# One pool pair for attention and experts, and a fill between indirect transfers in a row

## The chip, the cores and the metric

The kernel runs on one core of one Trainium2 chip. The metric is the device time of one execution in microseconds, the median of three runs. The engines are named as the profile names them: PE is TensorE's matrix multiply and PEld its weight load, DVE is VectorE, ACT is ScalarE, POOL is GpSimd, SP is the engine whose queue issues most plain DMA transfers. SBUF is the on-chip memory of 128 partitions; PSUM is the accumulator memory that TensorE writes, in banks of 512 f32 columns, eight of them.

## The reference

Two stages: a linear attention with a norm, and a mixture of eight experts in which each token goes to one expert.

```python
def _attn_ref(q, k, v, g_norm):            # q, k, v: 8 batches x 8 heads x 576 x 64
    kv = np.einsum('bhsd,bhse->bhde', k, v)
    out = np.einsum('bhsd,bhde->bhse', q, kv)
    rms = np.sqrt(np.mean(out * out, axis=-1, keepdims=True) + 1e-06)
    return (out / rms * g_norm).astype(np.float32)

def _moe_ref(x, w_gate, w1, w2):           # x: 4608 tokens x 512; 8 experts, 512 -> 1024 -> 512
    logits = x @ w_gate
    expert_idx = np.argmax(logits, axis=1)
    # gate_w: the softmax probability of the chosen expert
    for e in range(E):
        mask = expert_idx == e
        xe = x[mask]
        h = np.maximum(xe @ w1[e], 0.0)
        out[mask] = gate_w[mask, None] * (h @ w2[e])
```

## The kernel before

The kernel walks over 36 tiles of 128 tokens (`for s in range(36)`): products with q, norm, gate logits. Each finished row (512 f16 values, its token number and its gate weight) is sent to a scratch table in DRAM, sorted by expert, with an indirect DMA from GpSimd (`scatter`). Then each expert's rows come back with indirect DMAs, 128 rows at a time (`gather`), are transposed, go through both layers, and are sent to their places in the output with a third kind of indirect DMA (`put`). Each expert has up to five such tiles (`CT = 5`); rows beyond that form a "left" job at the end. For experts 0 and 1 the first three tiles (`AT = 3`) are done early, while the last scatters still run: these are `j0` and `j1`, and jobs 0 and 1 of the main loop are their remaining two tiles.

```python
def gather(xe, rows, src=None):
    return nc.gpsimd.indirect_dma_start(out=xe.bitcast(I32), in_=xs.ap() ..., in_offset=IndirectOffsetOnAxis(ap=rows, axis=0), ...)

def put(view, idx, ys):
    nc.gpsimd.indirect_dma_start(out=view, out_offset=IndirectOffsetOnAxis(ap=idx, axis=0), in_=ys, ...)
```

Attention and the early batches take their tiles from one SBUF pool and one PSUM pool:

```python
with (
    tc.manual_schedule(engines=by_hand),
    tc.tile_pool(name="pattn", bufs=1) as PA,
    tc.tile_pool(name="psattn", bufs=1, space=bass.MemoryType.PSUM) as PSA,
):
    ...                                     # attention, routing, j0, most of j1   (cut)
    W[2].stage1(hold=True)                  # loads of expert 2's weights, 2 MB each
    W[2].stage2(hold=True)
    for m in range(4):
        j1.one(m, ("op", "kvp")[m % 2])
        ...
    yp0 = PSA.tile([128, D], F32, tag="qtp", bufs=1, name="yp")
    j1.two(0, yp0)
    j1.done(0, yp0)                         # ys = yp * gate weight, then put(...)
    yp = PSA.tile([128, 2, D], F32, tag="kvp", bufs=1, name="yp")
    for t in (1, 2):
        j1.two(t, yp[:, t - 1, :])
        j1.done(t, yp[:, t - 1, :])
```

The experts use a second pair of pools, which takes over the memory of the first:

```python
with (
    tc.tile_pool(name="pffn", bufs=1) as PF,
    tc.tile_pool(name="psffn", bufs=1, space=bass.MemoryType.PSUM) as PSF,
):
    class Job:
        def flip(self, t):                  # transpose a gathered tile
            if t == 0:
                self.xt = PF.tile([128, 4, nt * 128], F16, tag=f"xt{nt}", bufs=2, name="xt")
                ...
            xp = PSF.tile([128, 4, 128], F16, tag="xp", bufs=2, name="xp")
            ...                             # 4 transposes on PE, a DVE copy xt <- xp, the row numbers
        def one(self, ws, f):               # first layer: 4 matmuls, then relu on ACT into ht
            hp = PSF.tile([128, wd], F32, tag="hp", bufs=3, name="hp")
            ...
        def two(self, t):                   # second layer: 8 matmuls, scaling on DVE, put on POOL
            yp = PSF.tile([128, D], F32, tag="yp", bufs=3, name="yp")
            ...
            ys = PF.tile([128, D], F32, tag="ys", bufs=8, name="ys")
            nc.vector.tensor_scalar(ys, yp, self.xe[t][:, 514:516].bitcast(F32), None, op0=ALU.mult)
            put(self.views[t], self.idx[:, t:t + 1], ys)

    with tc.manual_schedule(engines=by_hand):
        def next_row(n, t, job, ws, f):     # wait for a relu of this job, then gather for job n
            nc.gpsimd.tensor_copy(tick2, job.ht[:, f, c:c + 1])
            gather(jobs[n].xe[t], rowi[:, order[n], t:t + 1])

        for t in range(CT):
            gather(jobs[2].xe[t], rowi[:, 2, t:t + 1])
        for t in range(2):
            jobs[0].flip(t)
        for n in range(len(order)):
            for ws in range(job.halves):
                for f in range(8):
                    job.one(ws, f)
                    if coming and ...:      next_row(n + 2, coming.pop(0), job, ws, f)
                    if ws == job.halves - 1 and f >= 2 and flips:
                        nxt.flip(flips.pop(0))
                    ...                     # DVE: W[n + 1].half1, conversion of the next w1; SP: load of W[n + 2]
            for kk in range(max(job.nt, 4)):
                if kk < job.nt:
                    job.two(kk)
                ...                         # ACT: W[n + 1].half2, conversion of the next w2
                if n == 2 and kk == 1:
                    left_over_table()       # some 25 small DVE operations
```

Within one `manual_schedule` block each engine's order is that of the program. The two blocks are separate, and their orders are merged: the gathers of job 2, written after the puts of `j1`, stand before some of them in the GpSimd queue.

Of the kernel before, what the change touches and what calls it, by code (L numbers as in the profile page):

```python
# [28 lines left out]
def kernel(  # L29
# [165 lines left out]

    def gather(xe, rows, src=None):
        return nc.gpsimd.indirect_dma_start(  # L197
            out=xe.bitcast(I32),
            out_offset=None,
            in_=xs.ap() if src is None else src,  # L200
            in_offset=IndirectOffsetOnAxis(ap=rows, axis=0),
            bounds_check=E * N - 1,
            oob_is_err=False,
        )
# [8 lines left out]
    def put(view, idx, ys):  # L213
        nc.gpsimd.indirect_dma_start(  # L214
            out=view,
            out_offset=IndirectOffsetOnAxis(ap=idx, axis=0),
            in_=ys,
            in_offset=None,
            bounds_check=N - 1,
            oob_is_err=False,  # L220
        )
# [6 lines left out]
    with (  # L228
        tc.manual_schedule(engines=by_hand),
        tc.tile_pool(name="pattn", bufs=1) as PA,  # L230
        tc.tile_pool(name="psattn", bufs=1, space=bass.MemoryType.PSUM) as PSA,
    ):
# [43 lines left out]
        def heads(s):  # L276

            qp[s] = PA.tile([128, 2, 4, 64], F32, tag="qp", bufs=5, name="qp")
            (b0, j0), (b1, j1) = tokens(s)
            if b0 == b1:  # L280
                tv = ld["q", b0][:, :, 64 * j0:64 * j0 + 128]
                nc.gpsimd.tensor_copy(qp[s], tv.rearrange("p i (c d) -> p c i d", c=2))  # L282
            else:
                for c, (b, j) in enumerate(tokens(s)):
                    nc.gpsimd.tensor_copy(
                        qp[s][:, c, :, :], ld["q", b][:, :, 64 * j:64 * j + 64]
                    )
# [232 lines left out]
        class Route:  # L520
# [69 lines left out]
            def scatter(self, t):  # L590
                put_xs = nc.gpsimd.indirect_dma_start(  # L591
                    out=xs_views[9 * self.P + self.g0 + t],
                    out_offset=IndirectOffsetOnAxis(ap=self.sli[:, t:t + 1], axis=0),
                    in_=xgs[self.P, self.g0][:, t, :].bitcast(I32),
                    in_offset=None,
                )
                if self.P < 3:
                    known.append(put_xs.ins.name)
# [185 lines left out]
        yp0 = PSA.tile([128, D], F32, tag="qtp", bufs=1, name="yp")  # L784
        j1.two(0, yp0)
        j1.done(0, yp0)
        yp = PSA.tile([128, 2, D], F32, tag="kvp", bufs=1, name="yp")
        for t in (1, 2):
            j1.two(t, yp[:, t - 1, :])
            j1.done(t, yp[:, t - 1, :])  # L790


    with (
        tc.tile_pool(name="pffn", bufs=1) as PF,
        tc.tile_pool(name="psffn", bufs=1, space=bass.MemoryType.PSUM) as PSF,
    ):

        def left_over_table():

            ovr = PF.tile([128, 8], F32, tag="ovr")  # L800
            nc.vector.tensor_sub(ovr, cnt, dlt)
            nc.vector.tensor_scalar(ovr, ovr, float(CAP), 0.0, op0=ALU.subtract, op1=ALU.max)
            thr = PF.tile([128, 8, 32], F32, tag="thr")
# [4 lines left out]
            ov = PF.tile([128, 8], F32, tag="ov")  # L808
            nc.vector.reduce_sum(ov, thr, axis=AXX)
            oi = PF.tile([128, 8], F32, tag="oi")  # L810
            zero8 = PF.tile([128, 8], F32, tag="zero8")
            nc.vector.memset(zero8, 0.0)
            nc.vector.tensor_tensor_scan(oi, ov, zero8, 0.0, op0=ALU.add, op1=ALU.add)
            cm = PF.tile([128, 32, 8], F32, tag="thr")
            nc.vector.tensor_tensor(cm, _bc(oi, 1, 32), _bc(tcol, 2, 8), op=ALU.is_le)
            te = PF.tile([128, 32], F32, tag="te")
            nc.vector.reduce_sum(te, cm, axis=AXX)
            nc.vector.tensor_tensor(cm, cm, _bc(ov, 1, 32), op=ALU.mult)
            tk = PF.tile([128, 32], F32, tag="tk")
# [3 lines left out]
            e8 = PF.tile([128, 8], F32, tag="e8")  # L823
            nc.vector.tensor_scalar(e8, eoff, 1.0 / N, None, op0=ALU.mult)
            nc.vector.tensor_tensor(cm, _bc(te, 2, 8), _bc(e8, 1, 32), op=ALU.is_equal)
            cd = PF.tile([128, 32, 8], F32, tag="cd")
            nc.vector.tensor_tensor(cd, cm, _bc(dlt, 1, 32), op=ALU.mult)
            td = PF.tile([128, 32], F32, tag="td")
# [16 lines left out]

        class Job:


            def __init__(self, xe, w, okm, bgm, views):
# [3 lines left out]
                self.halves = 2 if self.cols > 512 else 1  # L853

            def flip(self, t):

                nt, xe = self.nt, self.xe
                if t == 0:
                    self.xt = PF.tile(
                        [128, 4, nt * 128], F16, tag=f"xt{nt}", bufs=2, name="xt"  # L860
                    )
                    self.idx = PF.tile([128, nt], I32, tag=f"idx{nt}", bufs=3, name="idx")
                xp = PSF.tile([128, 4, 128], F16, tag="xp", bufs=2, name="xp")
# [9 lines left out]
            def one(self, ws, f):  # L873
                if ws == 0 and f == 0:
                    self.ht = PF.tile(
                        [128, 8, self.cols], F16, tag=f"ht{self.nt}", bufs=2, name="ht"
                    )
                wd = self.cols // self.halves
                hp = PSF.tile([128, wd], F32, tag="hp", bufs=3, name="hp")
                for kk in range(4):  # L880
# [8 lines left out]
                    self.ht[:, f, ws * wd:(ws + 1) * wd], hp, ACTF.Relu  # L889
                )  # L890

            def two(self, t):
                yp = PSF.tile([128, D], F32, tag="yp", bufs=3, name="yp")
                for f in range(8):
                    nc.tensor.matmul(  # L895
                        yp, self.ht[:, f, t * 128:(t + 1) * 128], self.w.w2[:, f, :],
                        start=(f == 0), stop=(f == 7),
                    )
                ys = PF.tile([128, D], F32, tag="ys", bufs=8, name="ys")
# [5 lines left out]
        def left_over(t, t0, view):  # L905
# [5 lines left out]
            okm = PF.tile([128, 1], F32, tag="okm", bufs=2, name="okm")  # L911
            nc.vector.tensor_tensor(okm, pcol, nvf[:, bass.ds(t, 1)], op=ALU.is_lt)
            bgm = PF.tile([128, 1], F32, tag="bgm", bufs=2, name="bgm")
            nc.vector.tensor_scalar(bgm, okm, -BIG, BIG, op0=ALU.mult, op1=ALU.add)
            gi = PF.tile([128, 1], I32, tag="gi", bufs=2, name="gi")
# [7 lines left out]
        with tc.manual_schedule(engines=by_hand):  # L923
            jobs = []
            for n, e in enumerate(order):
                if e == "left":
                    jobs.append(None)
                    continue
                t0 = AT if n < 2 else 0
                x0 = 2 * AT + 2 * n if n < 2 else (10, 0, 5)[(n - 2) % 3]  # L930
                jobs.append(Job(
                    xe_bufs[x0:x0 + CT - t0], W[n], valid[:, e, t0:CT], bigm[:, e, t0:CT],
                    out_views[e * CT + t0:(e + 1) * CT],
                ))

            tick2 = PF.tile([128, 1], F16, tag="tick2")

            def next_row(n, t, job, ws, f):

                c = ws * (job.cols // job.halves)  # L940
                nc.gpsimd.tensor_copy(tick2, job.ht[:, f, c:c + 1])  # L941
                gather(jobs[n].xe[t], rowi[:, order[n], t:t + 1])

            for t in range(CT):
                gather(jobs[2].xe[t], rowi[:, 2, t:t + 1])
            for t in range(2):
                jobs[0].flip(t)

            for n in range(len(order)):
                job = jobs[n]  # L950
                if n == 4:
                    jobs[E] = left_over(0, 3 * CT, out_views[E * CT])
                    W[E] = jobs[E].w
                nxt = jobs[n + 1] if n + 1 < len(order) else None
                flips = list(range(nxt.nt)) if nxt is not None else []
                coming = list(range(CT)) if 0 < n < len(order) - 3 else []
                for ws in range(job.halves):
                    for f in range(8):
                        job.one(ws, f)
                        step = 8 * ws + f  # L960
                        if coming and (step % 3 == 0 if n > 1 else f < 5):
                            next_row(n + 2, coming.pop(0), job, ws, f)
                        if ws == job.halves - 1 and f >= 2 and flips:
                            nxt.flip(flips.pop(0))
                        if n > 0 and ws == 0 and f % 2 == 1 and nxt is not None:
                            W[n + 1].half1(nc.vector, f // 2)
                            if f == 7 and n + 2 < len(order):
                                W[n + 2].stage1()
                for kk in range(max(job.nt, 4)):
                    if kk < job.nt:  # L970
                        job.two(kk)
                    if n > 0 and kk < 4 and nxt is not None:
                        W[n + 1].half2(kk)
                        if kk == 3 and n + 2 < len(order):
                            W[n + 2].stage2()
                    if n == 2 and kk == 1:
                        left_over_table()

        nov = nc.values_load(tabi[0:1, 1, 7:8], min_val=0, max_val=NOV)
        with tc.If(nov > 1):  # L980
            with tc.For_i(1, nov) as t:
                job = left_over(t, 3 * CT, out_views[E * CT + 1])
                job.w.stage1()
                job.w.stage2()
                for kk in range(4):
                    job.w.half1(nc.vector, kk)
                    job.w.half2(kk)
                job.flip(0)
                for f in range(8):
                    job.one(0, f)  # L990
                job.two(0)
# [28 lines left out]
```

## Time and profile before

| | |
|---|---|
| time, median of 3 | 305.62 us (304.78 to 306.7) |
| span of the profiled execution | 328.7 us |
| busy: PE, PEld | 276.4 us (84%), 191.5 us (58%) |
| busy: DVE, ACT, POOL | 157.9 us (48%), 165.8 us (50%), 164.3 us (50%) |
| DMA moved | 85.73 MB, mean 261 GB/s |
| indirect transfers on POOL | 36 scatters to the table, 41 gathers (34, 6 and 1), 41 puts |

The profile is of one execution, which was longer than the timed ones. Busy shares are averages over stages with different limits: attention lasts until some 143 us, the early batches until 171, the experts from 180 on. Lines of the timeline have start and duration in us, engine, source line, operation, output and input, and in brackets the idle time of the engine before it with what ended it. "issue" is a wait that the profile shows no cause for; "remote" is a release whose origin the trace doesn't name. For an indirect DMA the line covers the work of GpSimd, not the landing of the data. In the chain of waits each piece is a start, a duration, and the work or transfer that was waited for.

### The profile page before, as it was taken

To read this page: it belongs to the slowest core of one execution; us is meant where nothing else is said; L and a number is where in the kernel's file an instruction comes from. 1 tells how busy PE (TensorE), PEld (TensorE's weight loads), DVE (VectorE), ACT (ScalarE), POOL (GpSimd) and SP (SyncE) were. 2 spreads that over 40 slices of the span, in tenths; PEclk is the share of its full clock that TensorE was granted. 3 is DMA by queue.
4 is the path that set the end of the run, shared out by engine and by line. 5 is a ranking of instruction groups with operands and counts; after the bars stand their busy time and mean duration, and the time that the engine had idled before them with its cause. 6 is when DMAs were issued, how large, how long until landed. Compare 5 with 4: busy or idle time off the path is not lost. (4 is left out here: it accounts for less than half of the span.)

```text
span 328.7 us, 7210 instructions
## 1 busy us (share of the span) xinstructions
PE 276.4 (84%) x2832; PEld 191.5 (58%) x2832; DVE 157.9 (48%) x424; ACT 165.8 (50%) x353; POOL 164.3 (50%) x238
## 2 busy tenths in 40 slices
PE   8897989979996967258952999799979999999992
PEld 3586877868885856224521665456446474665651
DVE  0034856844784747524321280787453354546130
ACT  1245766643764656427800356455434466473831
POOL 9511253764365663742773088327685484305051
PEclk9999999985999898769995899999997999999999
DMA  7999878949599767320695029997779597987330
GB/s 283 373 391 389 323 259 313 397 121 394 169 401 398 299 205 277 99 76 26 223 379 221 2 82 350 390 352 272 302 257 402 154 368 290 312 322 254 150 123 33
DMA packets 34883, 85.73 MB, mean 261 GB/s; under 512 B 3868, under 2 KB 4125, under 8 KB 34848
## 3 DMA queue, kind: packets, MB, share of 16 engines
q1 hardware_dynamic: 26592, 65.10, 54.9%
q0 software_dynamic: 6976, 18.96, 15.8%
q10 hardware_dynamic: 1280, 1.20, 1.1%
q8 instruction: 23, 0.38, 0.5%
q14 instruction: 12, 0.10, 0.1%
HBM read 71.71 MB, written 15.50 MB: 265 GB/s over the span
## 5 line engine op out<-in xcount | busy, mean ns | idle before, releaser
L888 ACT ACTIVATE ht<-hp 128x320 f16<-128x320 f32 (+2 forms) x120 | 49.1, 419 | 81.2 <-PE hp L881 70.4
L881 PE MATMUL hp<-xt,w1e 128*128 128x320 f16 (+2 forms) x480 | 72.2, 299 | 11.8 <-DVE xt L868 5.9
L214 POOL DMA_INDIRECT out_dram<-ys,idx x41 | 42.7, 1042 | 71.3 <-DVE ys L900 61.7
L881 PEld LDWEIGHTS <-w1e 128*128 128x128 f16 x480 | 45.7, 100 | 29.0 <-issue 7.4
L895 PE MATMUL yp<-w2e,ht 128*128 128x512 f16 x280 | 61.9, 379 | 0.0
L368 PE MATMUL op<-kvs,qts 128*128 128x144 f32 (+1 forms) x320 | 50.3, 315 | 3.2 <-DVE xg L408 1.9
L591 POOL DMA_INDIRECT xs_scratch<-xg,sli x36 | 35.4, 983 | 22.8 <-issue 22.2
L895 PEld LDWEIGHTS <-ht 128*128 128x128 f16 x280 | 27.3, 98 | 31.4
L368 PEld LDWEIGHTS op<-kvs,qts 128*128 128x128 f32 (+1 forms) x320 | 41.3, 193 | 6.8 <-DVE xg L408 2.3
L900 DVE TENSOR_SCALAR ys<-yp,xe 128x512 f32<-128x512 f32 x35 | 26.0, 750 | 39.9 <-PE yp L895 38.7
L197 POOL DMA_INDIRECT xe<-xs_scratch,rowi x34 | 35.7, 1049 | 9.4 <-issue 6.0
L394 DVE TENSOR_REDUCE ms<-sq 128x8 f32<-128x512 f32 x36 | 24.6, 684 | 22.0 <-ACT sq L389 18.4
L389 ACT ACTIVATE sq<-op 128x512 f32<-128x512 f32 x36 | 21.5, 596 | 25.6 <-PE op L368 22.6
L192 ACT CAST w2e<-ws 128x1024 f16<-128x1024 f32 x32 | 31.2, 1041 | 1.5 <-DMA ws<-in_moe_w_dram 1.5
L868 DVE COPY xt<-xp 128x512 f16<-128x512 f16 x35 | 14.7, 421 | 34.4 <-PE xp L865 21.1
L346 PE MATMUL qtp<-cf,qp 128*128 128x128 f32 x144 | 24.2, 293 | 1.5 <-POOL qp L282 1.5
L299 PE MATMUL kvp<-v,k 64*64 64x64 f32 x1152 | 24.4, 227 | 1.3 <-DMA v<-in_v_dram 0.7
L180 DVE TENSOR_SCALAR w1e<-ws,g 128x1024 f16<-128x1024 f32 x31 | 21.9, 755 | 6.8 <-DMA ws<-in_moe_w_dram 6.8
L408 DVE TENSOR_TENSOR xg<-op,rinv 128x512 f16<-128x512 f32 x36 | 24.5, 681 | 0.0
L299 PEld LDWEIGHTS kvp<-v,k 64*64 64x64 f32 x1152 | 20.3, 138 | 7.0 <-issue 7.0
L353 ACT COPY qts<-qtp 128x512 f32<-128x512 f32 x36 | 21.1, 585 | 6.4 <-PE qtp L346 6.3
L282 POOL COPY qp<-q 128x512 f32<-128x512 f32 x32 | 19.6, 626 | 9.3 <-DMA q<-in_q_dram 9.2
(115 smaller groups left out, 275.9 us busy)
## 6 DMA issues: line engine op xcount, KB each, us to landing
ws<-in_moe_w_dram SPq DMA_DIRECT2D x16, 2048.0 KB
q<-in_q_dram SPq DMA_DIRECT2D x8, 1152.0 KB
k<-in_k_dram SPq DMA_DIRECT2D x7, 1152.0 KB
v<-in_v_dram SPq DMA_DIRECT2D x7, 1152.0 KB
ws<-in_moe_w_dram SPq DMA_DIRECT2D x4, 1024.0 KB
k<-in_k_dram SPq DMA_DIRECT2D x2, 576.0 KB
v<-in_v_dram ACTq DMA_DIRECT2D x2, 576.0 KB
out_dram<-ys,idx POOLq DMA_INDIRECT x41
```

The lines of the kernel that those rows point to most:

```text
L192: copy(self.w2[:, 2 * kk:2 * kk + 2, :], self.s2[:, 2 * kk:2 * kk + 2, :])
L197: return nc.gpsimd.indirect_dma_start(out=xe.bitcast(I32), out_offset=None, in_=xs.ap() if src is None else src, in_offset=IndirectOffsetO ...
L214: nc.gpsimd.indirect_dma_start(out=view, out_offset=IndirectOffsetOnAxis(ap=idx, axis=0), in_=ys, in_offset=None, bounds_check=N - 1, oob_ ...
L299: nc.tensor.matmul(kvst[b][64 * ip:64 * ip + 64, c, 64 * i2:64 * i2 + 64], ld["k", b][ps, i, cs], ld["v", b][ps, i, cs], start=(j == 0), s ...
L368: nc.tensor.matmul(op[ts, c, 144 * i2:144 * i2 + 144], qts[s][:, 2 * i2 + c, ts], kvs[:, 2 * c + i2, :], start=True, stop=True,)
L394: nc.vector.reduce_sum(ms, sq, axis=AXX)
L408: nc.vector.tensor_tensor(xg[:, r, 0:512].rearrange("p (i h c n) -> p c i h n", c=2, i=2, h=2), ox, _bc(r4, 4, 64), op=ALU.mult,)
L591: put_xs = nc.gpsimd.indirect_dma_start(out=xs_views[9 * self.P + self.g0 + t], out_offset=IndirectOffsetOnAxis(ap=self.sli[:, t:t + 1], a ...
L881: nc.tensor.matmul(hp, self.w.w1[:, kk, f * 128:(f + 1) * 128], self.xt[:, kk, ws * wd:(ws + 1) * wd], start=(kk == 0), stop=(kk == 3),)
L888: nc.scalar.activation(self.ht[:, f, ws * wd:(ws + 1) * wd], hp, ACTF.Relu)
L895: nc.tensor.matmul(yp, self.ht[:, f, t * 128:(t + 1) * 128], self.w.w2[:, f, :], start=(f == 0), stop=(f == 7),)
L900: nc.vector.tensor_scalar(ys, yp, self.xe[t][:, 514:516].bitcast(F32), None, op0=ALU.mult)
```

## The change

It does two things. First, the second pair of pools goes away. The experts' tiles take turns in attention's buffers, under its tags, and all of it stands in one `manual_schedule` block, so the order on each engine is that of the program from start to end. The transposes of job 0 are placed before the last product of `j1`. Nothing has to be handed from pool to pool any more. Second, a function `spaced` puts a fill of 128x576 f16 on GpSimd between indirect transfers that follow one another; a call of `heads` (which itself has GpSimd copy a tile) resets it.

```diff
+    breath = P_const.tile([128, 576], F16, tag="breath")
+    near = []
+    def spaced():
+        if near:
+            nc.gpsimd.memset(breath, 0.0)
+        near[:] = [1]
     def gather(xe, rows, src=None):
+        spaced()
     def put(view, idx, ys):
+        spaced()
             def scatter(self, t):
+                spaced()
         def heads(s):
+            near.clear()
-    with (
-        tc.manual_schedule(engines=by_hand),
-        tc.tile_pool(name="pattn", bufs=1) as PA,
-        tc.tile_pool(name="psattn", bufs=1, space=bass.MemoryType.PSUM) as PSA,
-    ):
+    PA = ctx.enter_context(tc.tile_pool(name="pa", bufs=1))
+    PSA = ctx.enter_context(tc.tile_pool(name="psa", bufs=1, space=bass.MemoryType.PSUM))
+    with tc.manual_schedule(engines=by_hand):
 ...
-                    self.xt = PF.tile([128, 4, nt * 128], F16, tag=f"xt{nt}", bufs=2, name="xt")
-                xp = PSF.tile([128, 4, 128], F16, tag="xp", bufs=2, name="xp")
+                    self.xt = PA.tile([128, 4, nt * 128], F16, tag="k", bufs=2, name="xt")
+                if t % 2 == 0:
+                    self.xp = PSA.tile([128, 2, 8, 128], F16, tag="kvp", bufs=1, name="xp")
+                xp = self.xp[:, t % 2, 0:4, :]
 ...
-                if ws == 0 and f == 0:
-                    self.ht = PF.tile([128, 8, self.cols], F16, tag=f"ht{self.nt}", bufs=2, name="ht")
+                if ws == 0 and f % 4 == 0:
+                    self.ht.append(PA.tile([128, 4, self.cols], F16, tag="vq"[f // 4], bufs=2 + f // 4, name="ht"))
-                hp = PSF.tile([128, wd], F32, tag="hp", bufs=3, name="hp")
+                if f % 2 == 0:
+                    self.hp = PSA.tile([128, 2, 512], F32, tag="op", bufs=2, name="hp")
+                hp = self.hp[:, f % 2, 0:wd]
 ...
+        banks = ["qtp", "misc"]
-                yp = PSF.tile([128, D], F32, tag="yp", bufs=3, name="yp")
+                banks.reverse()
+                yp = PSA.tile([128, D], F32, tag=banks[0], bufs=1, name="yp")
-                ys = PF.tile([128, D], F32, tag="ys", bufs=8, name="ys")
+                ys = PA.tile([128, D], F32, tag="qp", bufs=5, name="ys")
 ...
-            for t in range(CT):
-                gather(jobs[2].xe[t], rowi[:, 2, t:t + 1])
-            for t in range(2):
-                jobs[0].flip(t)
+        for t in range(AT):
+            if t == 2:
+                for u in range(2):
+                    jobs[0].flip(u)
+            banks.reverse()
+            yp = PSA.tile([128, D], F32, tag=banks[0], bufs=1, name="yp")
+            j1.two(t, yp)
+            j1.done(t, yp)
+        for t in range(CT):
+            gather(jobs[2].xe[t], rowi[:, 2, t:t + 1])
```

The rest of the diff renames pools (`PF` to `PA`), moves lines to the outer block, and cuts the lines of `j1.two` that stood in the first block.

## The prediction

> **What bounds the kernel now.** I read the chain of waits first, because it tells which wait ends last. From 220 us to the end its pieces are the matmuls of the experts (`hp`, `yp`), with the GpSimd queue beside them. Its first pieces are something else:
>
> ```profile
> 173.82 1.00 DMA out_dram<-ys,idx
> 174.82 0.30 issue
> 175.12 3.03 DMA out_dram<-ys,idx
> ...
> 178.78 0.42 DVE xt L868
> ```
>
> The first copy into `xt`, a buffer of the second pair of pools, waits for the landing of the last scatter to the output, which reads `ys`, a buffer of the first pair. Neither needs the other's data: this is memory handed from one pool to the next. The timeline of the same stretch shows what it costs and why the scatter is so late:
>
> ```profile
> 157.80 1.05 POOL L197 DMA_INDIRECT xe<-xs_scratch,rowi  x1 [1.08 <-issue]
> ...
> 168.81 1.89 PE L505 MATMUL yp<-w2e,early 128*128 128x512 f16 x8 [1.88 <-issue]
> ...
> 172.34 0.75 DVE L512 TENSOR_SCALAR ys<-yp,xe 128x512 f32<-128x512 f32 x1 [3.59 <-remote]
> ...
> 175.12 0.98 POOL L214 DMA_INDIRECT out_dram<-ys,idx  x1 [0.30 <-issue]
> 178.78 0.42 DVE L868 COPY xt<-xp 128x512 f16<-128x512 f16 x1 [5.68 <-DMA out_dram<-ys,idx]
> ...
> 179.72 2.53 PE L881 MATMUL hp<-xt,w1e 128*128 128x256 f16 x11 [5.91 <-DVE xt L868]
> ```
>
> TensorE ends the early batches at 170.70 (168.81 + 1.89) and starts the next expert at 179.72, with eight transposes between: a hole of 9.0 us. Meanwhile GpSimd works through indirect transfers in a row, one each 1.31 us, five of them gathers that are not urgent (those of expert 2, first used at 190). Next the table of windows, for the clock (columns: busy time of PE, PEld, DVE, ACT, POOL, then the granted clock, DMA share, GB/s):
>
> ```profile
> 171.00:180.00 9.00, 0.94 (x10) 0.65 (x10) 1.76 (x5) 0.00 (x0) 4.01 (x4) 0.64 0.72 275
> 198.00:220.00 22.00, 19.41 (x127) 11.45 (x125) 11.49 (x32) 11.67 (x22) 11.53 (x15) 1.00 1.00 369
> 220.00:240.00 20.00, 18.89 (x126) 11.27 (x124) 12.52 (x31) 10.76 (x20) 12.48 (x16) 1.00 0.77 288
> 240.00:263.30 23.30, 20.68 (x127) 12.29 (x125) 9.65 (x23) 10.32 (x20) 13.26 (x17) 0.93 0.80 276
> 263.30:283.80 20.50, 19.92 (x136) 12.22 (x135) 10.32 (x21) 11.31 (x22) 12.62 (x17) 1.00 0.89 314
> 283.80:300.70 16.90, 16.90 (x115) 10.21 (x113) 7.88 (x18) 10.10 (x19) 4.38 (x5) 1.00 0.81 296
> 300.70:318.30 17.60, 17.60 (x110) 10.40 (x109) 6.99 (x11) 10.76 (x20) 4.72 (x5) 1.00 0.44 167
> ```
>
> Experts 6 and 7 take 16.9 and 17.6 us with TensorE full: that is what an expert of five tiles costs when nothing disturbs it. Experts 2 to 5 take 22.0, 20.0, 23.3 and 20.5. They are the ones in which GpSimd also gathers. Expert 2 is known to wait for weights (the chain has a load of 9.29 us there).
>
> One caution on scale: the profiled span is 328.7 us and the timed median 305.62. 23 us of what the trace shows isn't in the timed runs, and I can't say which.
>
> **What the Trainium skill says.** "TensorE: Matmul & The Clock Gate", section on the HAM clock gate, "What's actually happening": the array clock drops to half after an idle window of about 3.4 us and comes back after one of sustained work. The trace agrees: one-microsecond windows show 1.00 until 173, 0.50 from 174 to 182, and full clock 3.5 us after the restart at 179.72. "SBUF — State Buffer", section on the two separate sides: GpSimd and VectorE share a port pair as an exclusive lock, so a GpSimd fill can delay VectorE operations of certain kinds and the other way round. The trace hints at it: a small VectorE add of 0.16 us took 0.49 us beside a GpSimd copy at 66.1 us. "DMA: Bandwidth & Descriptors", section on the anatomy of a GpSimd DMA: about 2 us are fixed, mostly the wait for the write receipt. Here the last scatter took 3.03 us from start to landing, so 3 us is my figure.
>
> **The change part by part.**
>
> *One pool pair and one program order (gain).* `xt` moves to tag `k`, `ht` to `v` and `q`, `ys` stays in `qp`, transposes go to `kvp`, products to `op`, `qtp`, `misc`. The slots they need were freed by about 165 us (last use of staged weights 162.98, last relu of the early batches 164.4). The copy to `xt` no longer waits for any output scatter, and the transposes of expert 0 stand before the last early product, so they fill rather than follow. Expert 0 can start at about 170.7: minus 9.0 us. The clock then doesn't fall: expert 0 ran from 179.72 to 189.09 with its first 3.5 us at half speed, 1.75 us lost; with the transposes already done I count 2.0. Together minus 11.0.
>
> *The order costs something back.* The five gathers of expert 2 now stand behind all the early scatters, and each indirect transfer after the first has a fill ahead. The 128x516 f16 fills at the start took 517 ns each; 576 columns by the same rate, 0.55 us. A transfer in a row then takes 1.0 + 0.15 (the gap behind a small copy) + 0.55 = 1.70 us instead of 1.31. Counting from the first tail scatter at 153.2: seventeen transfers, the last starting at 153.2 + 16 x 1.70 = 180.4 and landing near 183.4. The fifth transpose for expert 2 would be due at about 182.2. About 1 us, or 2.5 if GpSimd comes to the tail already late from the fills before it; I take plus 1.8.
>
> *`yp` from three buffers to two (loss).* In expert 2 VectorE builds the table for left-over rows between the second and third scaling: 24 operations from 215.57 to 222.40. With three banks TensorE ran on. With two, the fifth product needs the bank of the third, which is read only after the table, at 222.40 + 0.75 = 223.15. Its natural start is 211.25 + 4 x 1.73 = 218.15. Plus 5.0 us, and the clock falls in that hole: half of 3.4 us, plus 1.7. Plus 6.7 together.
>
> *`xp` from two tiles to one tile of two halves (loss).* A third or fifth transpose now waits for the copy of the one before it, not of the one before that. Transposes start 0.76 us apart; a copy starts 0.42 after its transpose and takes 0.42, plus about 0.1 to be seen: 0.94. So 0.18 us, twice in each of six experts: plus 2.1.
>
> *`hp` as pairs.* Three banks become two pairs: the first of a pair waits for the same relu as before, the second for none. Zero.
>
> *The fills as load.* Per expert with gathers: five times (0.20 tick + 0.55 + 0.15 + 1.03) = 9.65 and five times 1.70 = 8.5, 18.2 us of GpSimd against 17.5 of TensorE. It is now about full, but gathers are issued a whole expert ahead, so the queue lags without being waited for. In the last two experts a fill fits in the 0.74 us that GpSimd idles between scatters. With port conflicts on VectorE: plus 1.0.
>
> *The fills as relief.* Where transfers follow in a row, other engines seem held: "remote" above (3.59 us, though the product had ended at 170.70), the same on ScalarE at 142.55 (3.13 us) in a row of thirteen, and the excess of experts 2 to 5 over 17.3 us: 4.7 + 2.7 + 6.0 + 3.2 = 16.6 us. That is what the fill must be for. But it sums to about the 23 us that timed runs don't show, and a 0.2 us tick copy already separates those gathers. If real and cured I guess 7 us; half a chance, minus 3.5.
>
> Sum: -11.0 + 1.8 + 6.7 + 2.1 + 1.0 - 3.5 = -2.9, so 302.7 us.
>
> **Rivals.** (1) *The fill is the real change.* For it: every ScalarE gap named "remote" in the attention stage (ending 70.44, 101.96, 117.19 us) has two indirect transfers just before, with at most a 0.2 us copy between. Against: the chain of GpSimd from 265.5 to 274 held nobody for the first 6 us. It would give 293 to 298. (2) *The two `yp` banks eat the gain* and the fills do nothing but load GpSimd: 305 to 309; for it, the table's 6.8 us stand in the trace in plain order. (3) *GpSimd becomes the bound*, its 18.2 us per expert pushing gathers behind the transposes: 310 to 316; against it, the expert of slack. (4) *The hole only moves*: weights of expert 3 are loaded only after those of expert 2 are converted, 9.29 us, so expert 2 waits the same; I have assumed that this load is issued earlier by the same 10 us, since its trigger, VectorE's fourth scaling in expert 1, moves too.
>
> **Range and chances.** Without relief the sum is 306.2, with full relief 299.2 and with an outsized one some 293; the saturated case gives 312. I take 302.5, 8 in 10 between 292 and 311. Faster by 2% means below 299.5: it needs the relief or a smaller table stall, 0.40. Above 311.7 needs rival 3, 0.15. Within 2%: 0.45.
>
> **What would show it.** The hole between the early `yp` and the first `hp` should shrink from 9.0 to under 2 us with the clock at 1.00 in it. A wait of `yp` for `ys` of about 5 us should appear once, in expert 2. Fills should take about 0.55 us, transfers in a row follow at 1.7. Experts 3 to 5 at 17 to 18 us would prove relief; at 20 to 23, none. I am wrong at the root if the hole stays (another buffer of the attention stage is held), or if the fifth product doesn't wait.

## The result, and the profile after

The changed kernel takes 340.57 us (median of four runs, 340.14 to 341.41) against 305.93 for the kernel before (304.78 to 306.70): a ratio of 1.1139, with a 95% interval of 1.1096 to 1.1183. It is 34.6 us slower. The prediction was 302.5, with a range of 292 to 311.

The waits of TensorE in the kernel after come first (columns: engine, what it ran and its line, the engine, tile and line it waited for; total us, times, longest):

```profile
PE hp L887 <- ACT ht L894: 24.7, 57, 0.6
PE xp L868 <- DMA xe<-xs_scratch,rowi: 7.1, 2, 5.7
PE yp L902 <- DVE ys L907: 5.3, 1, 5.3
```

The first line is new and large: a product of the first layer waits 57 times, up to 0.6 us each, for a relu. The third is the wait for the left-over table, which the prediction put at 5.0. The group of the fills, from the page of the kernel after:

```profile
L202 POOL MEMSET breath<- 128x576 f16 x94 | 57.0, 607 | 0.1
```

A fill takes 0.61 us (the working had 0.55; the rate that it names, 517 ns for 516 columns, gives 0.58), and there are 94. The timeline of the start of expert 6 shows what the wait looks like. No gather runs in this stage any more:

```profile
282.75 0.71 PE L887 MATMUL hp<-xt,w1e 128*128 128x320 f16 x4
283.57 0.44 ACT L894 ACTIVATE ht<-hp 128x320 f16<-128x320 f32 x1 [5.05 <-PE hp L887]
284.06 1.25 PE L887 MATMUL hp<-xt,w1e 128*128 128x320 f16 x8 [0.61 <-ACT ht L894]
...
285.83 1.25 PE L887 MATMUL hp<-xt,w1e 128*128 128x320 f16 x8 [0.53 <-ACT ht L894]
```

Four matmuls run into the first half of a pair. The second half is another bank and empty, and yet its four matmuls start only when the relu of the first half has ended. From then on the grouping is second half of one pair, first half of the next: eight matmuls in 1.25 us, then 0.53 us idle, a pair every 1.77 us. The compiled program says the same: the second group waits for the count of the relu on `hp[:, 0, :]`. The dependency is kept for the tile, not for its half.

The hole between the early batches and expert 0, on TensorE:

```profile
145.54 3.62 PE L516 MATMUL yp<-w2e,early 128*128 128x512 f16 x16
154.84 0.61 PE L868 MATMUL xp<-ch,xe 128*128 128x128 f16 x4 [5.68 <-DMA xe<-xs_scratch,rowi]
...
160.72 1.06 PE L887 MATMUL hp<-xt,w1e 128*128 128x256 f16 x4
```

It hasn't gone, it has another cause. TensorE stops at 149.2 and goes on at 154.84, now for the rows of expert 0 themselves; by 153 us the granted clock is at 0.50. GpSimd shows why, first in the timeline, then in the chain of waits:

```profile
143.40 1.00 POOL L225 DMA_INDIRECT out_dram<-ys,idx  x1 [0.17 <-issue]
...
145.15 1.00 POOL L225 DMA_INDIRECT out_dram<-ys,idx  x1 [0.17 <-issue]
```

```profile
141.46 5.28 DMA xs_scratch<-xg,sli
...
149.12 1.05 POOL xe L207
```

A row of transfers goes on at 1.75 us each, so the last scatter to the table starts only at 141.46. The first gather of expert 0 reads that table, and in the compiled program it waits for the landing of the scatters before it; it starts at 149.12, and the data are there at 154.84. The windows of experts 3 and more (start:end, length, busy us of PE, PEld, DVE, ACT, POOL with counts, granted clock, DMA share, GB/s) close the comparison, here experts 5 and 6:

```profile
259.40:282.75 23.35, 20.00 (x126) 11.37 (x125) 10.17 (x19) 10.77 (x20) 17.92 (x26) 1.00 0.76 256
282.75:306.10 23.35, 20.00 (x126) 11.38 (x125) 9.96 (x19) 10.77 (x20) 8.22 (x11) 1.00 0.65 236
```

Expert 5 still gathers and takes 23.35 us; expert 6 doesn't and takes the same, and expert 7 takes 22.9. From first product to first product, experts 6 and 7 of the kernel before take 18.4 and 17.6 (the window of 16.9 us in the prediction began 1.5 us inside expert 6, and that of expert 5 was too long by as much).

Theories. *Shared tile*: the two halves of `hp` wait for each other, 25 us or so. *Fills*: GpSimd is loaded and everything behind it late, most of the 35 us. *Two banks*: it is `yp`.

### The profile page after: what moved, and what is told of

It reads as the page before. It is cut to its first block, busy times and chain, and to the rows that moved or that the text cites. A ratio compares the mean times of both kernels' runs of the same rounds, so it can differ in the third digit from the quotient of the medians.

```text
span 339.6 us, 7304 instructions
## 1 busy us (share of the span) xinstructions
PE 280.1 (82%) x2832; PEld 185.9 (55%) x2832; DVE 168.3 (50%) x424; ACT 166.8 (49%) x353; POOL 221.6 (65%) x332
## 4 chain that ended last, share of the span: by engine, by line
PE 39%; POOL 16%; DMA 14%; issue 12%; ACT 10%; DVE 8%; POOLq 1%; SPq 0%; ACTq 0%
PE hp L887 13%; DMA out_dram<-ys,idx 9%; PE yp L902 8%; PE op L379 8%; POOL breath L202 6%; ACT ht L894 5%; PE kvp L310 4%; POOL xe L207 4%; POOL out_dram L225 3%; DMA q<-in_q_dram 3%; PE qtp L357 3%; POOL xs_scratch L603 2%; DVE ms L405 2%; DMA xs_scratch<-xg,sli 2%; ACT w2e L192 1%
## 5 line engine op out<-in xcount | busy, mean ns | idle before, releaser
L894 ACT ACTIVATE ht<-hp 128x320 f16<-128x320 f32 (+2 forms) x120 | 50.3, 420 | 110.3 <-PE hp L887 106.4
L887 PE MATMUL hp<-xt,w1e 128*128 128x320 f16 (+2 forms) x480 | 75.5, 293 | 24.9 <-ACT ht L894 24.7
L902 PE MATMUL yp<-w2e,ht 128*128 128x512 f16 x280 | 63.7, 386 | 5.3 <-DVE ys L907 5.3
L202 POOL MEMSET breath<- 128x576 f16 x94 | 57.0, 607 | 0.1
L379 PE MATMUL op<-kvs,qts 128*128 128x144 f32 (+1 forms) x320 | 47.5, 304 | 3.6 <-DVE xg L419 2.7
L603 POOL DMA_INDIRECT xs_scratch<-xg,sli x36 | 35.5, 986 | 11.3 <-issue 10.5
L379 PEld LDWEIGHTS op<-kvs,qts 128*128 128x128 f32 (+1 forms) x320 | 38.7, 183 | 7.1 <-DVE xg L419 3.2
L180 DVE TENSOR_SCALAR w1e<-ws,g 128x1024 f16<-128x1024 f32 x31 | 28.1, 951 | 5.1 <-DMA ws<-in_moe_w_dram 5.1
L357 PE MATMUL qtp<-cf,qp 128*128 128x128 f32 x144 | 22.8, 281 | 1.1 <-POOL qp L293 1.1
L310 PE MATMUL kvp<-v,k 64*64 64x64 f32 x1152 | 22.9, 223 | 1.0 <-DMA v<-in_v_dram 1.0
## 6 DMA issues: line engine op xcount, KB each, us to landing
ws<-in_moe_w_dram SPq DMA_DIRECT2D x16, 2048.0 KB, 11.5
ws<-in_moe_w_dram SPq DMA_DIRECT2D x4, 1024.0 KB, 10.6
```

The costliest lines, as they stand in the source:

```text
L202: nc.gpsimd.memset(breath, 0.0)
L310: nc.tensor.matmul(kvst[b][64 * ip:64 * ip + 64, c, 64 * i2:64 * i2 + 64], ld["k", b][ps, i, cs], ld["v", b][ps, i, cs], start=(j == 0), s ...
L357: nc.tensor.transpose(qtp[:, c, i2, :], qp[s][:, c, 2 * i2:2 * i2 + 2, :], ident)
L379: nc.tensor.matmul(op[ts, c, 144 * i2:144 * i2 + 144], qts[s][:, 2 * i2 + c, ts], kvs[:, 2 * c + i2, :], start=True, stop=True,)
L603: put_xs = nc.gpsimd.indirect_dma_start(out=xs_views[9 * self.P + self.g0 + t], out_offset=IndirectOffsetOnAxis(ap=self.sli[:, t:t + 1], a ...
L887: nc.tensor.matmul(hp, self.w.w1[:, kk, f * 128:(f + 1) * 128], self.xt[:, kk, ws * wd:(ws + 1) * wd], start=(kk == 0), stop=(kk == 3),)
```

## Experiments

All ratios are to the kernel before, run in turn with the variant on the same chip. Where two variants are compared in microseconds, the kernel before took the same within 2 us beside both.

**1. Tile or bank.** Two forms of the kernel before, with the same banks as after: four for `hp`, two for `yp`. In the first each `hp` is a tile, in the second two make one.

```
e1   hp = PSF.tile([128, wd], F32, tag="hp", bufs=4)             # yp: bufs=2
e2   if f % 2 == 0:                                              # yp: bufs=2
         self.hp = PSF.tile([128, 2, 512], F32, tag="hp", bufs=2)
     hp = self.hp[:, f % 2, 0:wd]
```

> The kernel before, with four hp tiles of one bank and two yp tiles instead of three and three. It uses the same eight banks in the same shares as the kernel after, but every hp is a tile of its own. Shared-tile theory (the second group of a pair waits for the relu of the first half of the same tile): no such wait here, only the wait for the table with two yp banks, 5.0 us and up to 1.7 of half clock: 306 + 5 to 7, so 311 to 313 us. Fill theory (the fills are what costs): 306 to 307 us. Two-bank theory (yp on two banks is what costs most of the 35 us): 330 us and more.

> The same as the run beside it, but the four hp banks are two tiles of two halves. Shared-tile theory: every second group waits 0.43 to 0.6 us for the relu of the first half; the trace after shows 24.7 us of it in 57 waits, so 311 to 313 plus 22 to 26: 333 to 339 us, and a wait of hp for ht in the table of waits of 20 us or more. Fill theory and two-bank theory: the same time as the run beside it, within 1 us.

Measured: 311.01 us (ratio 1.0179, 1.0132 to 1.0225) and 342.10 us (1.1229, 1.1187 to 1.1271). The same banks and the same instructions cost some 31 us more when two banks are one tile. The waits, first e1, then e2:

```profile
PE yp L895 <- DVE ys L900: 4.9, 1, 4.9
```

```profile
PE hp L883 <- ACT ht L890: 26.3, 59, 0.6
```

The large wait that e1 adds to the kernel before is the 4.9 us of `yp`; e2 has the same 4.9 and adds the relu. Neither has a fill, so the fill theory and the two-bank theory fall as main causes. The 31 us are more than the 22 to 26 expected, because the waits are not the whole price. The windows of expert 5, first e1, then e2:

```profile
249.50:267.94 18.44, 18.44 (x126) 11.30 (x124) 9.21 (x19) 10.77 (x20) 12.07 (x16) 1.00 0.91 327
259.73:283.08 23.35, 19.73 (x126) 11.38 (x125) 9.20 (x19) 10.76 (x20) 12.04 (x16) 1.00 0.74 257
```

Of the 4.9 us that the expert is longer, 3.6 are idle and 1.3 stand in TensorE's busy time, for the same 126 matmuls. Over the whole run TensorE is busy 277.7 us in e2 and 272.2 in e1: 5.5 us more, which with the 26.3 of waiting comes to about the difference.

**2. The wait taken away in the kernel after.** One relu for both halves:

```
-    nc.scalar.activation(ht[f // 4][:, f % 4, cols], hp, ACTF.Relu)
+    if f % 2 == 1:
+        nc.scalar.activation(ht[f // 4][:, f % 4 - 1:f % 4 + 1, cols],
+                             self.hp[:, :, 0:wd], ACTF.Relu)
```

> The kernel after, with one relu over both halves of a pair in place of one for each half; the tick copy that paces a gather then follows the odd half. Shared-tile theory: nothing reads a pair between its two groups, so the second group has nothing to wait for: 340.6 - 22 to 26, so 314 to 319 us, pairs 1.25 us apart in the last two experts. Fill theory: 338 to 341 us. Two-bank theory: 338 to 341 us.

Measured: 315.03 us (1.0343, 1.0266 to 1.0421), 25.5 less than the kernel after. As the shared-tile theory said.

**3. The kernel after without fills.** `spaced()` does nothing.

> The kernel after without a single fill between indirect transfers. Shared-tile theory: the fills stand off the path except where the gathers of expert 0 come late (waits of 5.68 and 1.46 us for xe); at most 7 us come back: 333 to 341 us. Fill theory: the fills cost most of the 35 us, so 306 to 315 us. If the fills bring relief in the timed runs, as half of the prediction assumed: slower than the kernel after, 342 to 348 us.

Measured: 330.88 us (1.0841, 1.0806 to 1.0877): 9.7 less than after, more than the 7 I allowed. TensorE at the entrance of expert 0:

```profile
148.38 0.39 PE L866 MATMUL xp<-ch,xe 128*128 128x128 f16 x4
...
151.66 0.60 PE L885 MATMUL hp<-xt,w1e 128*128 128x256 f16 x4
```

Expert 0 starts at 151.66, not at 160.72, and the hole is gone: so much of the prediction's first step holds as soon as the fills are out. 9.1 of the 9.7 us are here. The queue alone isn't all of it. Without fills the last scatter to the table starts at 136.07, 5.4 us earlier than with them, but the first gather of expert 0 at 139.94, 9.2 us earlier. Loads of weights are issued at 140.5 and 141.0 (141.1 and 141.6 with fills). From 135 to 137 us, when the last scatter of e4 runs, the DMA share is 0.22; with fills it is 1.02 to 1.05 from 145 to 155, where the same transfers now land. That the weights delay them is read from these numbers, not tested.

**4. Both, and the table.** One relu for a pair and no fills (e5); then also the table behind the fifth product of expert 2 (e6); or its 24 operations three at a time behind each product of experts 2 and 3 (e9):

```
-    if n == 2 and kk == 1: left_over_table()
e6   if n == 2 and kk == 4: left_over_table()
e9   if n in (2, 3):                 # table: a generator of 24 operations
         for _ in range(3): next(table, None)
```

> The kernel after with one relu for each pair and without the fills. If the shared tile (25.5 us) and the fills (9.7 us) act in different stretches, their effects add: 340.6 - 25.5 - 9.7 = 305.4, 303 to 308 us. If the fills cost time only because the experts were already held up, or the other way round, the sum doesn't hold: under 300 or over 310 us.

> The same with the table for the left-over rows built after the fifth product of expert 2 instead of after the second. Two-bank theory in its small form (the bank is held over the table, 4.9 to 5.5 us, and the clock falls in that hole): 5 to 7 us less than the run beside it, 297 to 301 us, no wait of yp for ys over 1 us, and faster than the kernel before by 4 to 8 us. If TensorE would only wait there for something else (weights of expert 3): 1 us less or none.

> One relu for each pair, no fills, and the 24 operations of the left-over table laid out three at a time behind each product of experts 2 and 3 instead of in one row. If the table costs what it shuts on VectorE (the bank of yp in one place, the conversion of the weights and the copies to xt in the other), it now fits in the holes of about 1 us between two scalings and costs nothing: 303.5 less 4.9 of wait and 1 to 2 of half clock, 296.5 to 298.5 us, with no wait of yp for ys and experts 2 and 3 at about 23 and 19 us. If expert 2 and 3 are held by the load of the weights all the same: 300 to 302 us, as with the table moved whole.

Measured: 303.49 us (0.9977, 0.9943 to 1.0010), 301.61 (0.9913, 0.9882 to 0.9944) and 296.24 (0.9757, 0.9686 to 0.9827). The two effects add, as e5 says (305.4 expected). Moving the table whole was a miss: 1.9 us instead of 5 to 7. The wait of `yp` is gone, but TensorE waits an expert later, in the timeline of e6:

```profile
198.82 2.73 DVE L180 TENSOR_SCALAR w1e<-ws,g 128x1024 f16<-128x1024 f32 x4
...
201.94 0.38 PE L866 MATMUL xp<-ch,xe 128*128 128x128 f16 x4 [4.05 <-DVE xt L869]
```

The conversion of weights and the copy to `xt` stand behind the table on VectorE. Spread out, it fits between two scalings: expert 3, with nine of the 24 operations, takes 18.97 us, as experts 4 to 6 do without any.

**5. The halves of `xp`.** The kernel before with its two `xp` tiles made one:

```
-    xp = PSF.tile([128, 4, 128], F16, tag="xp", bufs=2)
+    if t % 2 == 0:
+        self.xp = PSF.tile([128, 2, 8, 128], F16, tag="xp", bufs=1)
+    xp = self.xp[:, t % 2, 0:4, :]
```

> The kernel before with the two xp tiles as one tile of two halves, used once for each two transposes, and nothing else. The prediction gave 2.1 us: 0.18 us of wait at the third and the fifth transpose of an expert, as an odd one was taken to wait for nothing. Shared-tile theory: the odd transposes wait as well for the copy of the even half, and a product stands between two of them, so a wait counts once for each transpose after the first, four in an expert of five: 2 x 2.1 = 4.2, so 2 to 5 us more than before, 306.5 to 309.5 us. If TensorE has other work in those gaps: 304 to 305 us.

Measured: 310.93 us against 303.75 (1.0222, 1.0163 to 1.0280), 7.2 us, more than expected. The timeline of expert 5, in which the rows of expert 6 are transposed, first the kernel before in a second profile, then this one:

```profile
248.51 0.39 PE L865 MATMUL xp<-ch,xe 128*128 128x128 f16 x4
...
249.28 0.39 PE L865 MATMUL xp<-ch,xe 128*128 128x128 f16 x4
```

```profile
252.13 0.38 PE L867 MATMUL xp<-ch,xe 128*128 128x128 f16 x4
...
253.03 0.38 PE L867 MATMUL xp<-ch,xe 128*128 128x128 f16 x4
```

Transposes start 0.90 us apart instead of 0.77: 0.13 us at every transpose, 0.5 us in each expert, some 3 us in all. The rest lies in experts 2 and 3 (24.7 and 19.8 us against 23.2 and 18.6), where VectorE is late anyway. The two profiles are only 4.6 us apart, so the last 2 to 3 of the 7.2 us stay open.

Then the same cure as for `hp`: two transposes in a row and one copy of both, on top of e9.

```
+    for u in range(two):
+        for c in range(4):
+            nc.tensor.transpose(xp[:, u, c, :], xe[t + u][:, c * 128:c * 128 + 128], ident16)
+    nc.vector.tensor_copy(xt[:, :, t * 128:(t + two) * 128] as (p u c n), xp[:, 0:two, 0:4, :])
-    if ws == job.halves - 1 and f >= 2 and flips:
+    if ws == job.halves - 1 and f >= 3 and f % 2 == 1 and flips:
```

> The run with the table spread, and the transposes also by pairs: two transposes in a row into one tile, one copy of both, every second group. Each wait for a copy then falls away where a pair of products lies between. If the halves of xp cost 0.5 us for an expert (18.9 to 19.0 us an expert against 18.4 to 18.6 in the kernel before): 2 to 3 us less than the run with the table spread. If one copy twice as long holds the next pair as long as two did: the same within 1 us.

Measured: 289.20 us (0.9531, 0.9463 to 0.9600), 7 us less than e9, where 2 to 3 were expected. Experts 3 to 6 give 0.5 us each (18.44 against 18.97). Expert 2 gives 2.2 more (21.0 against 23.2), and expert 0 starts 2.2 earlier (149.94 against 152.13), which the expectation didn't count. The window of expert 5 in it:

```profile
223.50:242.00 18.50, 18.50 (x126) 11.32 (x125) 8.90 (x17) 9.40 (x12) 12.13 (x16) 1.00 0.93 326
```

TensorE is busy without a gap there. This version beats both kernels.

**6. What the fills do.** First the kernel before with the fills alone, and the kernel before unchanged for a second profile.

```
e7   def spaced():                   # called by gather, put and scatter
         if near: nc.gpsimd.memset(breath, 0.0)
         near[:] = [1]
```

> The kernel before with the fills and nothing else of the change. Queue theory (each fill lengthens a row of indirect transfers from 1.31 to 1.77 us, and what waits for the end of the row comes later): the first copy to xt waits for the last early scatter, some ten transfers after the tail, so 4 to 6 us, and a little from VectorE beside the fills: 309 to 313 us. Relief theory (the fills free other engines from holds by transfers in a row): 304 us or less. Neither: 305 to 306 us.

> The kernel before once more, unchanged, for its profile. Its profiled run took 330.6 us where its timed ones take 305. If transfers in a row hold the other engines whenever a profile is taken, this one takes 325 us or more again, with waits named remote and issue of 3 us and more at 134 to 143 us. If that one run was disturbed, it takes 304 to 309 us, and the first early product starts near 126 us as in the variant with four hp tiles.

Measured: 313.57 us for the fills alone (1.0318, 1.0256 to 1.0380); the queue theory. The first two transposes of expert 0 now wait 4.8 us for rows, and its first `hp` then waits 11.3 us for `xt`, against 8.6 without fills. The second profile of the kernel before took 306.71 us. Its first early product starts at 126.6 us, not at 143.19, and its experts 3 to 6 take 18.6, 18.5, 18.4 and 18.4 us. So the 20 to 23 us per expert, and every wait named "remote" that the prediction read, belong to that one first profile. Part 7 meets such waits again.

**7. Another order of the halves.** The kernel after without fills, all 120 relus kept, two tiles in turn (A first half, B first half, A second half, B second half):

```
-    if f % 2 == 0: self.hp = PSA.tile(...)
-    hp = self.hp[:, f % 2, 0:wd]
+    if f % 4 < 2: self.hps[f % 2] = PSA.tile(...)
+    hp = self.hps[f % 2][:, f % 4 // 2, 0:wd]
```

> The kernel after without fills, its 120 relus kept as they are, one for each half; only the halves are taken in another order: two tiles in turn, A first half, B first half, A second half, B second half. Shared-tile theory: another group of 0.54 to 0.65 us lies between the two groups of one tile, about as long as the relu and its signal (0.53 us of wait), so nearly all of the 25 us go although no instruction is saved: 304 to 309 us against 330.9. If the relu over both halves helped by lightening ScalarE (10 us less busy, 60 instructions fewer) and not by the missing wait: 328 to 331 us, with the waits of hp for ht still there.

Measured: 340.87 us, but the kernel before took 328.39 beside it, seven times between 327.8 and 330.0: a ratio of 1.0395 (1.0333 to 1.0457). It was another chip. Of the five that these runs met, three take 304 to 305 us for the kernel before and two take 328. The six runs after it settle what differs.

> The two tiles in turn, without fills, once more, beside the kernel before on the same chip. Where the kernel before takes about 305 us: shared-tile theory 304 to 309 us (ratio 1.00 to 1.01), relief of ScalarE theory 328 to 331 (ratio 1.08). Where the kernel before takes about 328 us: 339 to 343 us, as in the first run, with engines held in rows of indirect transfers.

> The run with the table spread and the transposes by pairs, without fills, as the partner of the run with fills on one chip. Where the kernel before takes about 305 us: ratio 0.95. Where it takes about 328 us, the held engines are not cured by anything in this version: 310 to 325 us.

> The same with the fills of the change. Where the kernel before takes about 305 us: the queue of GpSimd is later by 0.47 us for each transfer in a row, the hole before expert 0 comes back, 8 to 12 us more than the run without fills: 297 to 302. Where the kernel before takes about 328 us: relief theory says that the fills end the holds, so the same 297 to 302 us and 10 to 25 us less than without fills; without relief 8 to 12 us more than without fills.

These fell on a chip of the second kind (kernel before: 327.70). e13: 337.47 us (1.0272, 1.0169 to 1.0374). e14, the best version: 317.83 (0.9612, 0.9515 to 0.9710). e15, the same with fills: 308.59 (0.9435, 0.9344 to 0.9526). Two of the four executions of e14 lay 2% above its fastest and are not in its ratio; the other two took 313.61 and 315.59, so the fills save some 6 us here. All waits named "remote" in e14:

```profile
ACT early L508 <- remote: 5.1, 1, 5.1
DVE xt L895 <- remote: 5.0, 1, 5.0
ACT kvs L317 <- remote: 5.0, 2, 2.5
```

With the fills there is none, and the first early product starts at 130.3 instead of 137.6 us. But 10 to 25 us and a time of 297 to 302 were expected: the fills also bring the hole back, and TensorE waits 6.4 us for the rows of expert 0.

> The two tiles in turn, without fills. Where the kernel before takes about 305 us: shared-tile theory 304 to 309 us (the version with one relu for a pair, also without fills, took 303.5), relief of ScalarE theory 328 to 331. Where it takes about 328: 334 to 343, as twice before.

> The best version with fills. Where the kernel before takes about 305 us: 297 to 302 us, 8 to 12 us more than the 289.2 without fills, from the gathers of expert 0 that come late. Where it takes about 328 us: 306 to 311, as before.

> The kernel before with the fills only. Where the kernel before takes about 305 us: ratio 1.03, as before. Where it takes about 328 us: the fills end the holds but lengthen the queue; the best version came to 308.6 with them and 317.8 without, so 312 to 320 us here, a ratio under 0.98. Without relief 334 to 340.

These fell on a chip of the first kind (304.68). e16: 308.56 us (1.0146, 1.0070 to 1.0221), 22.3 less than e4, with 0.4 us of the wait of `hp` for `ht` left (24.9 in e4) and not one relu saved. So it is mainly the missing wait that helps, not a lighter ScalarE. e18: 305.05 (1.0030, 1.0002 to 1.0059), some 16 us more than e11 (on another chip of the first kind) where 8 to 12 were expected. Expert 0 starts at 157.2 instead of 149.9, and now the experts too wait for rows: GpSimd, with fills, is behind all the way.

```profile
PE xp L894 <- DMA xe<-xs_scratch,rowi: 5.8, 7, 1.9
```

e17, the fills alone again: 315.45 (1.0354, 1.0272 to 1.0435).

## Why the prediction was wrong

**The step that failed is "`hp` as pairs": "the first of a pair waits for the same relu as before, the second for none. Zero."** The second waits for the relu of the first, because both are one tile. e2 against e1 prices it at some 31 us in the kernel before, e3 at 25.5 in the kernel after. For `xp` the working had found half of this (the next use of a tile "now waits for the copy of the one before it"), but not that the second half waits as well, and it carried nothing over to `hp`. "PSUM — Partial Sum Buffer" of the Trainium skill, in the section on bank collisions, says to guard PSUM by bank and quadrant, not by address. The halves are two banks, so nothing of that kind asks for the wait, and e1 has the same banks as separate tiles without it; e2 shows that the program's own bookkeeping is coarser than the bank.

**"One pool pair and one program order", -11.0:** right in mechanism and size, without fills. In the second profile of the kernel before expert 0 still waits for the buffers of the first pools, here for 8.6 us:

```profile
163.69 2.74 PE L881 MATMUL hp<-xt,w1e 128*128 128x256 f16 x12 [8.56 <-DVE xt L868]
```

In e4 it starts at 151.66, 12.0 us earlier, without that wait. With the fills 3.0 are left. No run takes the one pool pair without the new order, so the 12.0 are the worth of both together. The clock's part was read a little short: in the first profile the windows show 0.50 up to 183 us and 0.60 from 183 to 184, so full clock came back some 4 us after the restart at 179.72, not 3.5.

**"The order costs something back" +1.8 and "the fills as load" +1.0:** mis-sized. The delay was worked out for the gathers of expert 2; it is those of expert 0 that come first in need. Measured 9.7 (e4), 9.1 (e7), 11.5 (e3 against e5). The time of a transfer in a row was right: 1.70 forecast, 1.75 measured.

**"`yp` from three buffers to two", +6.7:** right. In the kernel after the wait is 5.3 us, and the mean clock from 207 to 214 us 0.52. In e1 the wait is 4.9 us and the time 5.5 (from the ratio).

**"`xp`", +2.1:** the wait per transpose was about right (0.13 for 0.18 us), but counted twice per expert where it comes four times, and what it does in the experts where VectorE is late was left out: 7.2 us (e10).

**"The fills as relief", -3.5:** on chips of the first kind nothing. The working named the doubt itself (23 us that timed runs don't show) and yet gave it half a chance, and rival 1 a place. On the second kind the relief is real.

The measured terms, each from its own surroundings: -12.0 + 25.5 + 5.5 + 7.2 + 9.7 = 35.9, beside 34.6 for the whole. Of the rivals, (2) was right for its 5 us, and (3) happens in part where TensorE is fast enough (e18). (4) didn't happen: the conversion of expert 3's weights, which stands in expert 2 and waits for their load, starts 10.6 us earlier in e4 and waits no longer, so the load moved with the rest. First the kernel before in its second profile, then e4:

```profile
188.96 2.79 DVE L180 TENSOR_SCALAR w1e<-ws,g 128x1024 f16<-128x1024 f32 x4 [6.50 <-DMA ws<-in_moe_w_dram]
178.33 2.82 DVE L180 TENSOR_SCALAR w1e<-ws,g 128x1024 f16<-128x1024 f32 x4 [5.70 <-DMA ws<-in_moe_w_dram]
```

## What to carry to other kernels

Before you join several buffers into one tile, list who writes and who reads each part: what is tracked for the whole tile makes its halves wait for each other, even in different banks. Either read the tile once, both halves together, or put other work between its halves. Each thing added to an engine's queue, however far from the critical path, is to be followed to the first transfer behind it that somebody needs, and to what else moves data at the time when that transfer now runs. And if the profiled run is 8% longer than the timed ones, don't derive gains from its gaps: profile again first.

## What the runs showed of the hardware

Chips differ for this program: about 305 us on three of them, 325 to 330 on two, for the kernel before. Only one of the five was met at two times, with about 305 us at both, so it is likely but not shown that the chip decides and not the hour. On the second kind engines stand still while GpSimd issues indirect transfers in rows: waits named "remote" of up to 5.5 us (e12), and the first early product 11 to 17 us later than the 126 us of the first kind (137.6 in e14, 140.6 in e12, 143.19 in the first profile, whose chip isn't on record but which looks the same). A fill of 0.6 us between two transfers ended them (e15). That it is the row that holds the engines is read from the traces and from this cure; what in the chip holds them wasn't found. The kernel after, as it is, was not run on a chip of the second kind, nor a shorter fill on either.

Beside the fills, VectorE's conversions of weights (128x1024) took longer. The kernel after, then the same without fills (e4):

```profile
L180 DVE TENSOR_SCALAR w1e<-ws,g 128x1024 f16<-128x1024 f32 x31 | 28.1, 951 | 5.1 <-DMA ws<-in_moe_w_dram 5.1
L180 DVE TENSOR_SCALAR w1e<-ws,g 128x1024 f16<-128x1024 f32 x31 | 22.0, 758 | 5.7 <-DMA ws<-in_moe_w_dram 5.7
```

The kernel before shows it too: 1001 ns with the fills alone (e7), 758 without (e8). VectorE's scalings of `yp`, which read PSUM, take 750 ns with and without. "SBUF — State Buffer" of the Trainium skill, in the section on the two separate sides, has GpSimd and VectorE share a port pair; the numbers agree with that, though no run shows that it is the ports.
